# GpSimd's pieces of each head tied to scales, and the order of the hash codes' transfers, in a bucketed attention with two expert layers

## The chip, the cores and the metric

The kernel runs on one core of one Trainium2 chip. The metric is the device time of one execution in microseconds (us). TensorE is PE in the rows, VectorE is DVE, ScalarE is ACT, GpSimd is POOL, and SyncE, which issues nearly all transfers, is SP.

## The reference, cut to what matters

Sixteen attention heads (2 batches of 8, 768 tokens, 64 wide) come first. A query may attend only to keys of its own bucket; the bucket is the sign pattern of six projections. Two expert layers follow.

```python
q_bits = (np.einsum('bhsd,dk->bhsk', q, proj) > 0)   # k_bits likewise
mask = q_bucket[:, :, :, None] == k_bucket[:, :, None, :]
scores = np.where(mask, scale * np.matmul(q, k.T), -1e9)
attn = softmax(scores); attn_out = np.matmul(attn, v)
x = moe(attn_out)            # top-1 of 8 experts, relu, gates
return (x @ w_a) * (x @ w_b) @ w_out
```

## The kernel before

The program is written out by hand: within an engine, instructions run in the order of the code. The attention loop runs over `g`, 96 steps of one head `h` (0 to 15) and one tile `t` (0 to 5) of 128 queries. Step `g` issues the scores of tile `g + 1` (`scores`, L183 and L184: for each half of the keys one matmul with the rounded values and the codes, `tq` and `tk`, and one with the corrections, `bq` and `bk`), then `smax` on VectorE: a minimum over the scores in PSUM (L189, `mm`) and a two-input instruction that makes from it the scale and bias of the exponential (L190, `sb`; "a scale" below). ScalarE takes the exponential (L198, `p`), TensorE transposes it in two halves (L211, `tp`), and ScalarE or VectorE copies each half out (`pt`, L215 and L217). The product with the values (`av`, L226) and the output step of an older head (`o_out`, L265 to L293: matmul `m`, then `lp`, `xf` or `x_b` on VectorE) lie between.

`side(pos)` is called three times in a step (positions 0, 1, 2). It makes the operands of coming heads at places that the table `K` gives as pairs (tile, position). For a head two ahead: `split_a` rounds on ScalarE (`tq`, `tk`, L110), `split_b` makes the corrections. Of the queries, the first half is a VectorE instruction (`bq`, L123) and the second a GpSimd cast (L127). Of the keys, the first half is a GpSimd subtraction (`bk`, L129) and the second a GpSimd cast (L130). GpSimd has more work: the sums of the router's logits (`lg`, L290) and the repacking of the head's output into 16-bit planes (`x_q`, L247, from `to_planes` and `late_planes`), both at the end of `o_out` in tile 4. A `held` copy (L842, L845) reads the newest scale, so that what follows it on GpSimd starts only when that scale is made. Before, the query cast at (5, 2) stands behind one, and the key subtraction at (2, 2) behind none.

The codes: eight small matmuls (L149) give the projections of the next head, one VectorE instruction (L164, `code`) compares them, and `hash_codes` (L159 to L172) sends the result in eight transfers of 9 KB from SP's queue into twelve rows of `tq` and `tk` (L171), four for the queries and then four for the keys. In heads 0 and 1 it is four transfers of 18 KB. From step 62 on a list `todo` gives VectorE one piece of the first batch's router per step (`s1`, `s1b`, ...: L316 to L398), directly behind `smax`; from head 11 tile 3 on it holds the six scatters of the first batch (L482, `xr`), issued by GpSimd. While heads 14 and 15 run, `extra` hands GpSimd pieces of the expert layer, each behind a held copy (L744, L753).

Of the kernel before, what the change touches and what calls it, by code (L numbers as in the profile page):

```python
# [7 lines left out]
F32 = mybir.dt.float32  # L8
# [7 lines left out]
ALU = mybir.AluOpType  # L16
# [5 lines left out]
S, D, NB, NH = 768, 64, 2, 8  # L22
# [1 line left out]
N, DM, E, FF, F2 = 1536, 512, 8, 1024, 1536  # L24
C = 224
GR = ((0, 6), (6, 4), (10, 2))
K = {'se': (2, 0, 2, 0, 2, 0), 'se0': (0, 1, 2, 1, 1, 2), 'ev': (0, 0, 0, 1, 0, 1, 0, 0, 0, 0, 1, 0), 'ev0': (0, 0, 0, 1, 0, 1, 0, 0, 0, 1, 0, 0), 'ev1': (0, 0, 0, 1, 0, 1, 0, 0, 0, 1, 0, 1), 'avl': (5,), 'oul': 0, 'hml': 0, 'hc': ((0, 0), (0, 2), (1, 1), (2, 1)), 'sa': (None, (2, 2)), 'sb': ((1, 0), (2, 2)), 'sa0': ((2, 2), (4, 1)), 'sb0': ((3, 2), (5, 0)), 'hm0': 0, 'hc0': ((1, 0), (1, 2), (3, 0), (4, 1))}
C_ID, C_TRI, C_THR, C_REV, C_TOK, C_IOTA, C_BASE, C_SLOT = 0, 128, 256, 258, 266, 278, 279, 287
CW = C_SLOT + C
FAR = 1024.0  # L30
# [4 lines left out]
def attn_moe_kernel(ctx: ExitStack, tc: tile.TileContext, xin, cst, projd, wblk, wmoe, w2in, out):  # L35
    nc = tc.nc
    PE, ACT, DVE, POOL = nc.tensor, nc.scalar, nc.vector, nc.gpsimd
# [22 lines left out]
    lg = const.tile([128, 12, 16], F32, name="lg")  # L60
# [3 lines left out]
    pos = const.tile([128, 12], F32, name="pos")  # L64
# [25 lines left out]
    NHD = NB * NH  # L90
    X, XT, V, T, B, PT = {}, {}, {}, {}, {}, {}
    st, pt_ = {}, {}
    scl, nbs, last = {}, {}, {}
# [20 lines left out]
    def split_b(h, i, lo=0, n=S, parts=(0, 1)):  # L114
        copy = POOL.tensor_copy if h or i else ACT.copy
        x = X[h][:, i * S + lo:i * S + lo + n]
        if (h, i) not in B:
            B[h, i] = tb.tile([128, S], F32R, tag="b" + "qk"[i], name="b" + "qk"[i])
        b = B[h, i][:, lo:lo + n]
        t = T[h, i].bitcast(F32)[:, lo:lo + n]  # L120
        if i == 0:
            if 0 in parts:
                DVE.scalar_tensor_tensor(  # L123
                    out=b[:64], in0=x[:64], scalar=-0.125, in1=t[:64], op0=ALU.mult, op1=ALU.subtract
                )
            if 1 in parts:
                copy(b[64:], t[64:])  # L127
        else:
            (POOL if h else DVE).tensor_tensor(out=b[64:], in0=x[64:], in1=t[64:], op=ALU.subtract)  # L129
            copy(b[:64], t[:64])  # L130

    hp_ = {}

# [27 lines left out]
    def hash_codes(h):  # L161
        n = 192 if h > 1 else 384
        c = sm.tile([128, n], F32R, tag="code" if h > 1 else "o", name="code", bufs=1 if h > 1 else 2)
        DVE.tensor_scalar(  # L164
            out=c, in0=hp_[h, 0][:, :n], scalar1=thr[:, 0:1], scalar2=thr[:, 1:2], op0=ALU.is_gt, op1=ALU.mult
        )
        for j in range(4):
            i, k = divmod(j, 2)
            for r in range(384 // n):
                at = r * 384 + k * n  # L170
                nc.sync.dma_start(  # L171
                    out=T[h, i].bitcast(F32)[64:76, at:at + n],  # L172
                    in_=c.bitcast(F32)[32 * j + 12 * r:32 * j + 12 * r + 12],
                )

    def scores(g):
# [64 lines left out]
    def halves(ap):  # L241

        return ap.bitcast(U16).rearrange("p t (n a) -> p t a n", a=2)

    def to_planes(t0, nt, hh, src):
        o = x_q.bitcast(U16).rearrange("p t (a n) -> p t a n", a=2)[:, t0:t0 + nt, :, hh * 64:(hh + 1) * 64]
        POOL.tensor_copy(o, src)  # L247

    def late_planes(hh, t0=0, nt=6):
        to_planes(t0, nt, hh, halves(x_b)[:, t0:t0 + nt, :, hh * 64:(hh + 1) * 64])  # L250

    oT, rs = {}, {}

    def o_evac(h, q=None, copy=DVE.tensor_copy):
        n = q[1] * 128 if q else 384
# [9 lines left out]
    def o_out(h, q=None):  # L265
        b, hh = divmod(h, NH)
        o, r = oT.pop((h, q)), rs.pop((h, q))
        p = ps_m.tile([128, 512], F32, tag="m", name="m")
        t0, nt = q or (0, NT)
        t = slice(b * 6 + t0, b * 6 + t0 + nt)  # L270
        lp = sm.tile([128, nt, 16], F32, tag=f"lp{nt}", name="lp", bufs=2) if hh else lg[:, t]
        if b:
            xo = x_b[:, t0:t0 + nt, hh * 64:(hh + 1) * 64]
        else:
            xf = xo = sm.tile([128, 6, 64], F32, tag="xf", name="xf", bufs=1)
        if q is None:
            for j in range(3):
                PE.matmul(p[:, j * 160:(j + 1) * 160], o[:, j * 128:(j + 1) * 128], wb[:, hh], start=True, stop=True)
            ps = p[:, :480].rearrange("p (j c n) -> p j c n", j=3, c=2)
            rr = r.rearrange("p (c j) -> p j c", c=2).unsqueeze(3)  # L280
            lo, xo, sh = lp.rearrange("p (c j) n -> p j c n", c=2), xo.rearrange("p (c j) n -> p j c n", c=2), [128, 3, 2]
        else:
            for j in range(nt):
                PE.matmul(p[:, j * 80:(j + 1) * 80], o[:, j * 128:(j + 1) * 128], wl, start=True, stop=True)
            ps = p[:, :nt * 80].rearrange("p (j n) -> p j n", j=nt)
            rr, lo, sh = r[:, :nt].unsqueeze(2), lp, [128, nt]
        DVE.tensor_tensor(out=lo, in0=ps[..., 64:], in1=rr.to_broadcast(sh + [16]), op=ALU.mult)
        DVE.tensor_tensor(out=xo, in0=ps[..., :64], in1=rr.to_broadcast(sh + [64]), op=ALU.mult)
        if hh:
            (DVE if hh >= NH - 2 else POOL).tensor_tensor(out=lg[:, t], in0=lg[:, t], in1=lp, op=ALU.add)  # L290
        if not b:
            to_planes(0, 6, hh, halves(xf))
        elif NH + 3 <= h < L:  # L293
            late_planes(hh)

    def router(gi):
        t0, n = GR[gi]
# [362 lines left out]
    with tc.manual_schedule():  # L660
# [19 lines left out]
        for r, c in ((0, 0), (64, 12)):  # L680
            p = pst[r:r + 64]
            DVE.tensor_copy(p[:, c + 38:c + 44], p[:, c:c + 6])
            for to in (6, 32):
                DVE.tensor_scalar(
                    out=p[:, c + to:c + to + 6], in0=p[:, c:c + 6], scalar1=-1.0, scalar2=None, op0=ALU.mult
# [53 lines left out]
        held = sm.tile([128, 1], F32, tag="held", name="held", bufs=1)  # L739
        L = NHD - 1  # L740
# [29 lines left out]
        for g in range(NG):  # L770
# [57 lines left out]
            def side(pos):  # L828
                if (t, pos) == (5, 0) and h and h + 3 < NHD:
                    split_a(h + 3, 0)  # L830
                if g + 1 < NG and K["se" if 0 < h < L else "se0"][t] == pos:
                    sexp(g + 1)
                if h < L and (t, pos) == (1, 0):
                    hash_codes(h + 1)
                    if 0 < h < L - 1:
                        load_halves(h + 2)
                for i in range(2):
                    if h + 2 < NHD and K["sa" if h > 1 else "sa0"][i] == (t, pos):
                        split_a(h + 2, i)
                    if h + 2 < NHD and K["sb" if h > 1 else "sb0"][i] == (t, pos):  # L840
                        if t == 5:
                            POOL.tensor_copy(held, last[0])  # L842
                        split_b(h + 2, i, parts=(0,) if h > 1 and i == 0 else (0, 1))
                if (t, pos) == (5, 2) and h and h + 3 < NHD:
                    POOL.tensor_copy(held, last[0])  # L845
                    split_b(h + 3, 0, parts=(1,))

            side(0)
            tposes(g, 0)
# [694 lines left out]
```

## Time and profile before

| | us |
|---|---|
| median of 3 runs | 726.84 (726.68 to 727.46) |
| the profiled execution | 729.09 |
| its span, first to last instruction | 727.3 |
| TensorE busy | 705.2 |
| VectorE busy | 554.6 |
| ScalarE busy | 448.9 |
| GpSimd busy | 276.2 |

The profile is of one execution. Times in its rows run from the first instruction. A row of the timeline is a start, a length, the engine, the line of the kernel, the operation, what it writes and reads, the shape and a count; a bracket behind it is the idle time of the engine just before and what ended it. Rows that follow each other may be merged into one with a count. Matmuls are pipelined, so their lengths overlap, and the distance of starts says more than the length. The attention stage lasts until about 262 us, and the granted clock of TensorE is 1.00 in each of its stretches.

### The profile page before, as it was taken

The numbers are of one execution on the slowest core, as the hardware profiler recorded it, in microseconds if no ns is written. First come the engines' busy times: TensorE is split into PE (matmuls) and PEld (weight loads), VectorE is DVE, ScalarE is ACT, GpSimd is POOL, SyncE is SP. The second block draws the span as 40 slices with busy tenths as digits, with TensorE's granted clock in tenths as the row PEclk, the third lists the DMA queues.
The fourth block names the chain that finished last, engine by engine and source line by source line (L and its number), as shares of the span: only waits on it lengthen the run. The fifth ranks groups of instructions, "written<-read, shape, count | busy, mean of one in ns | idle before, by whom it ended". The sixth has DMA issues, their size and how long they took to land.

```text
span 727.3 us, 13315 instructions
## 1 busy us (share of the span) xinstructions
PE 705.2 (97%) x4505; PEld 602.5 (83%) x4506; DVE 554.6 (76%) x1108; ACT 448.9 (62%) x962; POOL 276.2 (38%) x328
## 2 busy tenths in 40 slices
PE   8899999999999999999999999999999999999995
PEld 6666776776666588999999999999999999999994
DVE  6777777778777787788888878886887877777644
ACT  5887788777777536677778766566443453444320
POOL 4342233222445447854454303234322333223234
PEclk9999999999999999999999999999999999999998
DMA  7345465542331039699899741133211222121013
GB/s 246 110 140 197 155 227 183 171 140 82 125 93 48 30 122 249 162 243 229 217 288 252 245 133 35 54 115 88 59 58 59 87 68 79 50 67 59 0 57 120
DMA packets 57017, 93.52 MB, mean 129 GB/s; under 512 B 20864, under 2 KB 25072, under 8 KB 56944
## 3 DMA queue, kind: packets, MB, share of 16 engines
q1 hardware_dynamic: 54192, 86.12, 40.3%
q0 software_dynamic: 2304, 6.31, 2.3%
q8 instruction: 37, 0.61, 0.3%
q14 instruction: 36, 0.29, 0.1%
q10 hardware_dynamic: 448, 0.20, 0.1%
HBM read 75.16 MB, written 13.12 MB: 121 GB/s over the span
## 4 chain that ended last, share of the span: by engine, by line
PE 73%; DVE 5%; POOL 5%; issue 5%; DMA 5%; SPq 3%; ACT 3%; ACTq 0%; DVEq 0%; POOLq 0%
PE tp L211 6%; PE av L226 6%; PE y L1071 5%; PE aba L1308 3%; PE abb L1308 3%; PE aba L1310 3%; PE aba L1309 3%; PE s L183 3%; PE abb L1310 3%; PE abb L1309 3%; PE h L1033 3%; PE h L1032 3%; PE h L1031 3%; SPq L171 3%; PE s L184 3%
## 5 line engine op out<-in xcount | busy, mean ns | idle before, releaser
L189 DVE TENSOR_REDUCE mm<-s 128x1 f32<-128x768 f32 x96 | 91.1, 949 | 29.0 <-PE s L184 27.3
L198 ACT ACTIVATE p<-s,sb 128x768 f32<-128x768 f32 x96 | 95.0, 990 | 24.1 <-DVE sb L190 21.3
L211 PEld LDWEIGHTS tp<-cs,p 128*128 128x128 f32 x576 | 64.0, 140 | 40.1 <-ACT p L198 24.8
L211 PE MATMUL tp<-cs,p 128*128 128x128 f32 x576 | 82.4, 279 | 7.3 <-ACT p L198 4.1
L539 DVE TENSOR_TENSOR wl<-wr,wh 128x512 fp32r<-128x512 f32 x125 | 82.1, 697 | 4.6 <-ACT wh L538 0.8
L215 ACT ACTIVATE pt<-tp 128x384 f32<-128x384 f32 x143 | 65.1, 488 | 32.6 <-PE tp L211 32.6
L1002 POOL TENSOR_TENSOR pc<-t,pc 128x256 fp32r<-128x256 f32 x38 | 32.8, 865 | 134.9 <-ACT pc L1001 119.8
L1071 PE MATMUL y<-hl,wh 128*128 128x448 f32 x224 | 75.1, 378 | 1.0 <-DVE hl L1045 0.9
L183 PE MATMUL s<-tk,tq 76*128 76x384 f32 x192 | 74.0, 385 | 1.8 <-DMA tk<-code 0.8
L538 ACT ACTIVATE wh<-wr 128x512 fp32r<-128x512 f32 x128 | 73.5, 624 | 0.6 <-DMA wr<-wmoe 0.5
L1031 PE MATMUL h<-xh,wh 128*128 128x224 f32 x256 | 70.4, 275 | 1.0 <-ACT xh L1027 0.8
L1032 PE MATMUL h<-xl,wh 128*128 128x224 f32 x256 | 70.4, 275 | 0.6 <-DVE xl L1028 0.3
L1033 PE MATMUL h<-xh,wl 128*128 128x224 f32 x256 | 70.6, 276 | 0.0
L226 PE MATMUL av<-pt,v 128*64 128x384 f32 x360 | 68.0, 499 | 0.2 <-DVE r L261 0.2
L184 PE MATMUL s<-bk,bq 128*128 128x384 f32 x192 | 65.2, 339 | 0.0
L129 POOL TENSOR_TENSOR bk<-x,tk 64x768 fp32r<-64x768 f32 x15 | 27.3, 1820 | 90.9 <-ACT tk L110 90.6
L1072 PE MATMUL y<-hl,wl 128*128 128x224 f32 x224 | 59.6, 266 | 0.0
L1031 PEld LDWEIGHTS h<-xh,wh 128*128 128x128 f32 x256 | 49.0, 191 | 2.4 <-ACT xh L1027 1.0
L1002 POOL TENSOR_TENSOR pc<-s,pc 128x256 fp32r<-128x256 f32 x44 | 37.8, 869 | 33.1 <-ACT pc L1001 31.4
L952 ACT ACTIVATE x<-r 128x512 uint8<-128x512 uint8 x36 | 28.5, 793 | 34.7 <-DVE x L949 34.7
L1032 PEld LDWEIGHTS h<-xl,wh 128*128 128x128 f32 x256 | 49.2, 192 | 0.9 <-DVE xl L473 0.5
L1198 ACT ACTIVATE gh<-p 128x384 fp32r<-128x384 f32 x21 | 11.0, 526 | 62.6 <-DVE p L1327 62.6
(266 smaller groups left out, 1982.0 us busy)
## 6 DMA issues: line engine op xcount, KB each, us to landing
wr<-wmoe SPq DMA_DIRECT2D x128, 256.0 KB
r<-w2in SPq DMA_DIRECT2D x36, 512.0 KB
x<-xin SPq DMA_DIRECT2D x30, 384.0 KB
xr<-zero SPq DMA_DIRECT2D x13, 512.0 KB
xt<-xin SPq DMA_DIRECT2D x14, 384.0 KB
v<-xin SPq DMA_DIRECT2D x16, 192.0 KB
tq<-code SPq DMA_DIRECT2D x56, 9.0 KB
tk<-code SPq DMA_DIRECT2D x56, 9.0 KB
```

The source lines that it names most:

```text
L183: PE.matmul(p[:, c, :384], T[h, 0][:76, qs], T[h, 1][:76, sl], start=True, stop=False)
L184: PE.matmul(p[:, c, :384], B[h, 0][:, qs], B[h, 1][:, sl], start=False, stop=True)
L189: DVE.tensor_reduce(out=m[:, 1:2], in_=st[g][:, :, :384], axis=AX.XY, op=ALU.min)
L198: ACT.activation(p.rearrange("p (c n) -> p c n", c=2), st.pop(g)[:, :, :384], ACTF.Exp, scale=scl.pop(g), bias=nbs.pop(g), accum_out=sums[ ...
L211: PE.transpose(ps[:, j * 128:(j + 1) * 128], pt_[g][:, k * 128:(k + 1) * 128], ident)
L226: PE.matmul(av[h][c * 64:(c + 1) * 64, :384], v, PT[h][:, k, c * 384:(c + 1) * 384], start=(k == 0), stop=(k == NT - 1), skip_group_check= ...
L538: ACT.activation(h, r, ACTF.Copy)
L539: eng.tensor_tensor(out=l, in0=r, in1=h.bitcast(F32), op=ALU.subtract)
L1031: PE.matmul(ps, wh, xh, start=first, stop=False)
L1032: PE.matmul(ps, wh, xl, start=False, stop=False)
L1033: PE.matmul(ps, wl, xh, start=False, stop=last)
L1071: PE.matmul(p, wh[:, w], hl, start=(f == 0), stop=False, skip_group_check=True)
```

## The change

It has two parts.

The transfers of the codes: the four of the keys go first. Of the queries' four, those for columns 0 to 191 and 192 to 383 follow and those for 384 to 575 and 576 to 767 are last. Their number and size stay.

GpSimd's pieces: from head 2 on, the subtraction for the keys moves from (2, 2) to (3, 0), behind a held copy. The keys' cast, which followed it at once, moves to (4, 0), behind a held copy of its own, and the sum of the logits follows it. The repacking of the output moves from tile 4 to (5, 2), behind the held copy there and ahead of the queries' cast; heads 0 and 1 get that held copy too. From head 13 on, sums and repacking stay in `o_out`.

```diff
-'sb': ((1, 0), (2, 2))
+'sb': ((1, 0), (3, 0))
...
         else:
-            (POOL if h else DVE).tensor_tensor(out=b[64:], in0=x[64:], in1=t[64:], op=ALU.subtract)
-            copy(b[:64], t[:64])
+            if 0 in parts:
+                (POOL if h else DVE).tensor_tensor(out=b[64:], in0=x[64:], in1=t[64:], op=ALU.subtract)
+            if 1 in parts:
+                copy(b[:64], t[:64])
...
-        for j in range(4):
-            i, k = divmod(j, 2)
-            for r in range(384 // n):
+        for j in (2, 3, 0, 1) if n == 384 else (2, 3, 0, 1, 4, 5):
+            i, k = divmod(j % 4, 2)
+            for r in (range(384 // n) if j in (2, 3) else (j // 4,)):
...
+        add, turn = [], []
         if hh:
-            (DVE if hh >= NH - 2 else POOL).tensor_tensor(out=lg[:, t], in0=lg[:, t], in1=lp, op=ALU.add)
+            add = [lambda: (DVE if hh >= NH - 2 else POOL).tensor_tensor(out=lg[:, t], in0=lg[:, t], in1=lp, op=ALU.add)]
         if not b:
-            to_planes(0, 6, hh, halves(xf))
+            turn = [lambda: to_planes(0, 6, hh, halves(xf))]
         elif NH + 3 <= h < L:
-            late_planes(hh)
+            turn = [lambda: late_planes(hh)]
+        if h < NHD - 3:
+            adds.extend(add)
+            turns.extend(turn)
+        else:
+            for f in add + turn:
+                f()
...
-                        if t == 5:
+                        if (t, i) in ((5, 1), (3, 1)):
                             POOL.tensor_copy(held, last[0])
-                        split_b(h + 2, i, parts=(0,) if h > 1 and i == 0 else (0, 1))
-                if (t, pos) == (5, 2) and h and h + 3 < NHD:
+                        split_b(h + 2, i, parts=(0,) if h > 1 else (0, 1))
+                if 1 < h < NHD - 2 and (t, pos) == (4, 0):
                     POOL.tensor_copy(held, last[0])
-                    split_b(h + 3, 0, parts=(1,))
+                    split_b(h + 2, 1, parts=(1,))
+                    if adds:
+                        adds.pop()()
+                if (t, pos) == (5, 2) and h < L:
+                    POOL.tensor_copy(held, last[0])
+                    for f in adds + turns:
+                        f()
+                    adds.clear()
+                    turns.clear()
+                    if h and h + 3 < NHD:
+                        split_b(h + 3, 0, parts=(1,))
```

What stands in a row, at three places. First SP's queue, one steady head (`x` and `v` are a later head's inputs, `xt` the input of the code matmuls, `xr<-zero` a clearing of memory). Before:

```order
L98 DMA x<-xin 128x768 x2
L100 DMA v<-xin 128x384
L171 DMA tq<-code 12x192 x4
L171 DMA tk<-code 12x192 x4
L105 DMA xt<-xin 128x768
L782 DMA xr<-zero 256x1x512 x2
```

The same place after:

```order
L98 DMA x<-xin 128x768 x2
L100 DMA v<-xin 128x384
L173 DMA tk<-code 12x192 x4
L173 DMA tq<-code 12x192 x4
L105 DMA xt<-xin 128x768
L791 DMA xr<-zero 256x1x512 x2
```

Only the two groups of four have changed places.

Second GpSimd, one steady head. Before:

```order
L845 COPY held<-sb 128x1
L127 CAST bq<-tq 64x768
L129 TENSOR_TENSOR bk<-x,tk 64x768
L130 CAST bk<-tk 64x768
L290 TENSOR_TENSOR lg<-lg,lp 128x96
L247 COPY x_q<-xf 128x12x64
```

After:

```order
L859 COPY held<-sb 128x1
L249 COPY x_q<-xf 128x12x64
L127 CAST bq<-tq 64x768
L851 COPY held<-sb 128x1
L130 TENSOR_TENSOR bk<-x,tk 64x768
L854 COPY held<-sb 128x1
L132 CAST bk<-tk 64x768
L293 TENSOR_TENSOR lg<-lg,lp 128x96
```

Two held copies are new, subtraction and cast are parted by one of them, and the repacking stands ahead of the queries' cast.

Third GpSimd from the end of head 10 to head 12, where the scatters begin (`L482 DMA xr` before, `L491 DMA xr` after). Before:

```order
L845 COPY held<-sb 128x1
L127 CAST bq<-tq 64x768
L129 TENSOR_TENSOR bk<-x,tk 64x768
L130 CAST bk<-tk 64x768
L482 DMA xr<-x_q,pos_i 3328x512
L290 TENSOR_TENSOR lg<-lg,lp 128x96
L482 DMA xr<-x_q,pos_i 3328x512
L845 COPY held<-sb 128x1
L127 CAST bq<-tq 64x768
L482 DMA xr<-x_q,pos_i 3328x512
L129 TENSOR_TENSOR bk<-x,tk 64x768
```

After:

```order
L859 COPY held<-sb 128x1
L127 CAST bq<-tq 64x768
L491 DMA xr<-x_q,pos_i 3328x512
L851 COPY held<-sb 128x1
L130 TENSOR_TENSOR bk<-x,tk 64x768
L854 COPY held<-sb 128x1
L132 CAST bk<-tk 64x768
L293 TENSOR_TENSOR lg<-lg,lp 128x96
L491 DMA xr<-x_q,pos_i 3328x512
L859 COPY held<-sb 128x1
L127 CAST bq<-tq 64x768
L491 DMA xr<-x_q,pos_i 3328x512 x2
```

The first scatter now stands ahead of head 11's subtraction, and two scatters stand ahead of head 12's.

## Rows read from the trace of the kernel before

**Rows 1.** Windows by head: length; PE, PEld, DVE, ACT, POOL busy; clock; DMA.

```profile
41.81:56.09 14.28, 14.28 (x100) 10.21 (x99) 10.95 (x23) 11.46 (x23) 5.46 (x8) 1.00 0.57 185
56.09:70.95 14.86, 14.48 (x100) 10.20 (x99) 10.98 (x23) 11.56 (x23) 4.85 (x6) 1.00 0.51 168
...
158.99:175.22 16.23, 14.71 (x108) 10.43 (x107) 13.90 (x29) 11.68 (x23) 3.65 (x4) 1.00 0.28 91
175.22:191.42 16.20, 14.75 (x100) 10.21 (x99) 13.04 (x30) 11.49 (x23) 5.35 (x6) 1.00 0.37 122
```

**Rows 2.** Timeline of PE: scores inside a head, then at two heads' starts.

```profile
55.45 0.34 PE L184 MATMUL s<-bk,bq 128*128 128x384 f32 x1
55.64 0.34 PE L183 MATMUL s<-tk,tq 76*128 76x384 f32 x1
...
65.38 0.34 PE L184 MATMUL s<-bk,bq 128*128 128x384 f32 x1
66.11 0.42 PE L183 MATMUL s<-tk,tq 76*128 76x384 f32 x1 [0.38 <-DMA tk<-code]
...
229.94 0.34 PE L184 MATMUL s<-bk,bq 128*128 128x384 f32 x1
230.38 0.41 PE L183 MATMUL s<-tk,tq 76*128 76x384 f32 x1
```

**Rows 3.** Chain that ended last (start, length, what): the last code transfer.

```profile
107.52 0.71 SPq L171
108.28 1.83 DMA tk<-code
```

**Rows 4.** Timeline of PE: the two long stalls, heads 10 and 11.

```profile
169.12 0.93 PE L211 MATMUL tp<-cs,p 128*128 128x128 f32 x6 [1.52 <-ACT pt L215]
...
185.52 0.93 PE L211 MATMUL tp<-cs,p 128*128 128x128 f32 x6 [1.44 <-ACT pt L215]
```

**Rows 5.** Timeline of DVE: scales, a router instruction, the scatter's addresses.

```profile
109.12 0.48 DVE L190 SCALAR_TENSOR_TENSOR sb<-mm 128x2 f32<-128x2 f32 x1
...
165.73 1.76 DVE L190 SCALAR_TENSOR_TENSOR sb<-mm 128x2 f32<-128x2 f32 x1
...
167.64 0.78 DVE L322 TENSOR_TENSOR oh<-rt_cd,rt_cm 128x48 bf16<-128x48 f32 x1
...
180.45 0.17 DVE L386 TENSOR_TENSOR pos_i<-pos,rt_p 128x6 int32<-128x6 f32 x1
...
182.08 1.81 DVE L190 SCALAR_TENSOR_TENSOR sb<-mm 128x2 f32<-128x2 f32 x1
...
188.26 0.16 DVE L190 SCALAR_TENSOR_TENSOR sb<-mm 128x2 f32<-128x2 f32 x1
```

**Rows 6.** Timeline of POOL: a query cast, a key subtraction, a scatter and its waiter.

```profile
112.41 0.83 POOL L127 CAST bq<-tq 64x768 fp32r<-64x768 f32 x1
...
165.65 1.82 POOL L129 TENSOR_TENSOR bk<-x,tk 64x768 fp32r<-64x768 f32 x1 [8.35 <-ACT tk L110]
...
186.66 0.99 POOL L482 DMA_INDIRECT xr<-x_q,pos_i  x1 [0.17 <-issue]
...
192.37 0.82 POOL L127 CAST bq<-tq 64x768 fp32r<-64x768 f32 x1 [3.70 <-DMA xr<-x_q,pos_i]
```

**Rows 7.** Timeline of DVE across a steady head's start.

```profile
111.94 0.16 DVE L190 SCALAR_TENSOR_TENSOR sb<-mm 128x2 f32<-128x2 f32 x1
112.80 0.56 DVE L217 COPY pt<-tp 128x384 f32<-128x384 f32 x1 [0.69 <-PE tp L211]
```

**Rows 8.** Timeline of ACT at the same place: exponentials of tiles 0 and 1.

```profile
112.22 0.99 ACT L198 ACTIVATE p<-s,sb 128x768 f32<-128x768 f32 x1 [0.45 <-DVE sb L190]
...
115.31 0.99 ACT L198 ACTIVATE p<-s,sb 128x768 f32<-128x768 f32 x1 [0.28 <-DVE sb L190]
```

**Rows 9.** Timeline of PE at the same place: their transposes.

```profile
113.64 0.82 PE L211 MATMUL tp<-cs,p 128*128 128x128 f32 x6
...
117.00 0.88 PE L211 MATMUL tp<-cs,p 128*128 128x128 f32 x6
```

More of the change, by code (lines that the diff above doesn't have):

```diff
@@ L26 @@
 GR = ((0, 6), (6, 4), (10, 2))
-K = {'se': (2, 0, 2, 0, 2, 0), 'se0': (0, 1, 2, 1, 1, 2), 'ev': (0, 0, 0, 1, 0, 1, 0, 0, 0, 0, 1, 0), 'ev0': (0, 0, 0, 1, 0, 1, 0, 0, 0, 1, 0, 0), 'ev1': (0, 0, 0, 1, 0, 1, 0, 0, 0, 1, 0, 1), 'avl': (5,), 'oul': 0, 'hml': 0, 'hc': ((0, 0), (0, 2), (1, 1), (2, 1)), 'sa': (None, (2, 2)), 'sb': ((1, 0), (2, 2)), 'sa0': ((2, 2), (4, 1)), 'sb0': ((3, 2), (5, 0)), 'hm0': 0, 'hc0': ((1, 0), (1, 2), (3, 0), (4, 1))}
+K = {'se': (2, 0, 2, 0, 2, 0), 'se0': (0, 1, 2, 1, 1, 2), 'ev': (0, 0, 0, 1, 0, 1, 0, 0, 0, 0, 1, 0), 'ev0': (0, 0, 0, 1, 0, 1, 0, 0, 0, 1, 0, 0), 'ev1': (0, 0, 0, 1, 0, 1, 0, 0, 0, 1, 0, 1), 'avl': (5,), 'oul': 0, 'hml': 0, 'hc': ((0, 0), (0, 2), (1, 1), (2, 1)), 'sa': (None, (2, 2)), 'sb': ((1, 0), (3, 0)), 'sa0': ((2, 2), (4, 1)), 'sb0': ((3, 2), (5, 0)), 'hm0': 0, 'hc0': ((1, 0), (1, 2), (3, 0), (4, 1))}
 C_ID, C_TRI, C_THR, C_REV, C_TOK, C_IOTA, C_BASE, C_SLOT = 0, 128, 256, 258, 266, 278, 279, 287
@@ L172, in hash_codes @@
                     out=T[h, i].bitcast(F32)[64:76, at:at + n],
-                    in_=c.bitcast(F32)[32 * j + 12 * r:32 * j + 12 * r + 12],
+                    in_=c.bitcast(F32)[32 * (j % 4) + 12 * r:32 * (j % 4) + 12 * r + 12],
                 )
@@ L250, in late_planes @@
         to_planes(t0, nt, hh, halves(x_b)[:, t0:t0 + nt, :, hh * 64:(hh + 1) * 64])
-    oT, rs = {}, {}
+    oT, rs, adds, turns = {}, {}, [], []
     def o_evac(h, q=None, copy=DVE.tensor_copy):
```

## The prediction

> **What bounds the kernel now.** I read first the windows cut at the code matmul of each head, then TensorE's timeline in the long heads, then who was late there. In a good head TensorE has no free time: 14.28 us long, 14.28 us busy, with VectorE at 10.95 and ScalarE at 11.46 [rows 1]. So only what makes a head longer than 14.28 can be won, and only in the attention stage. Two kinds of loss stand out.
>
> The first is at the start of a head. The third score matmul of tile 0, the first that reads the second half of the keys' codes, follows its forerunner by 0.73 us where 0.19 is usual, and what ended the wait is a transfer of `tk` codes [rows 2]. The head around that row is 14.86 us long [rows 1]; nine heads' starts have such a loss.
>
> The second is in heads 10 and 11, 16.23 and 16.20 us long [rows 1]. In each TensorE stands idle once before a transpose, 1.52 and 1.44 us [rows 4]. The row names a `pt` copy as the releaser, but the transpose needs the exponential `p`, and that needs the scale. The scale at that point takes 1.76 and 1.81 us instead of 0.16 [rows 5, 7]. In head 10 GpSimd's subtraction for the keys started 0.08 us ahead of it, at 165.65, and ends at 167.47; the scale ends at 167.49 [rows 5, 6]. So a scale that comes while GpSimd computes waits until the GpSimd instruction is done. In steady heads the same happens with the shorter cast, 0.48 us [rows 5], and TensorE loses nothing there. Copies out of PSUM are not held: one of 0.56 us runs beside a cast [rows 6, 7].
>
> **The change part by part.** *The codes.* The code transfers leave SP's queue 0.76 us apart, and the last lands 1.83 us after its issue [rows 3]. Before, the first scores of a head need the seventh transfer (columns 0 to 383 of the keys' codes) and the eighth. After, they need the four of the keys and the fifth; the built program has them wait for these five alone, and the sixth to eighth are waited for by later tiles. The last one that tile 0 needs thus comes 3 x 0.76 = 2.3 us earlier. The largest loss at a head's start is under 0.6 us, so all of them should go, with 1.7 us to spare. Their size: measured on the starts of the score matmuls, the nine losses, from 0.54 at 66.11 (0.73 - 0.19) to 0.25 at 230.38 (0.44 - 0.19) [rows 2], add up to 3.0. The bounds are 0 and 9 times the first head's 0.58 (14.86 - 14.28 [rows 1]), 5.2; the sum of what was measured is the value to take. What is late next is nothing that a row shows: VectorE and ScalarE have 3 us free in such a head [rows 1]. Heads 0 and 1 have no code wait and win nothing. The queue's other transfers keep their places.
>
> *The subtraction behind a scale.* In head 10 the subtraction would start about 0.3 us after the scale ends (a held copy and the start; between scale and cast at 111.94 and 112.41 it is 0.47 from start to start [rows 6, 7]). The scale is then free, and the 1.52 us go [rows 4]. Two scales of a steady head are 2.8 us apart (109.12 and 111.94 [rows 5, 7]), and the subtraction lasts 1.82 [rows 6], so it fits between them. I put down 1.5; bounds 0 (it meets the next scale instead) and 1.9 (16.23 - 14.28 [rows 1]).
>
> In head 11 the scale is freed as well, 1.4 us [rows 4], but the subtraction now stands behind the first scatter, and the built program has it wait for the scatter's landing. Addresses are ready at 180.6 [rows 5], so the scatter is issued at 180.8 or so. From issue to the next waiting instruction's start took 5.7 us for the second scatter (186.66 to 192.37 [rows 6]), my nearest row. So the subtraction would run at about 186.5 to 188.3 instead of 182.05. The next scale is that of head 12's tile 0, at 188.26 [rows 5], which without the stall comes 1.4 us sooner, at 186.9. It would be held for some 1.4 us. What of that reaches TensorE: at a steady start the scale ends at 112.10, the exponential starts 0.12 later and is done at 113.2, and the transpose starts at 113.64 [rows 7 to 9], which leaves 0.4. So up to 1.0 us comes back; if the scatter lands sooner or later than the scale, none. I put down 0.6, hence 0.8 gained in head 11. Bounds: 1.4 and 0.
>
> In head 12 the subtraction waits for two scatters in the same way and may meet another scale; before, its cast waited likewise and TensorE lost nothing that I can see. I put down 0.2 lost, bounds 0 and 1.6.
>
> *The other pieces.* The new held copies lie on GpSimd, which is busy 4.85 us in 14.86 [rows 1]: nothing, as long as it has that much free time. The cast behind the next scale removes the 0.48 us scale [rows 5], worth nothing since TensorE did not wait. Repacking and query cast behind head `h + 1`'s first scale take 2 x 0.83 [rows 6] and end some 2.1 us behind it; the next exponential is 3.1 us behind the first (112.22 and 115.31 [rows 8]). Readers of all these operands come a head or more later, and the load of a later head's `x`, which waits in SP's queue for the subtraction, is delayed in heads 11 and 12 alone, a full head before its use. In the last two heads GpSimd's list only changes the place of one sum and one repacking; I put down nothing.
>
> **A rule against it.** The row first: the router instruction `oh` in head 10, a VectorE instruction with two inputs, took 0.78 us from 167.64, while the keys' cast ran behind the subtraction that ended at 167.47 [rows 5, 6]; its end, 168.42, is about one cast (0.83 [rows 6]) later. The router stands directly behind the scale, and so, after the change, does the subtraction. The Trainium skill (GPSIMD Engine Reference, section 8, Key points) says that GpSimd contends with VectorE instructions with two SBUF inputs or in a two-port mode. By that rule, with which the trace agrees on `oh`, the pieces right behind a scale can hold the router's instructions instead of the scale. By the rule head 10's 1.5 could be lost and the sum be 3.6; without it the sum is 5.1 as below. The third rival works the mechanism out from rows.
>
> **The sum.** 3.0 + 1.5 + 0.8 - 0.2 = 5.1 us. The profiled execution took 729.09 us, a span of 727.3 and 1.8 around it; 729.09 - 5.1 = 724.0. It was 2.25 us above the median of the runs, and the median becomes 726.84 - 5.1 = 721.7. Behind the attention stage everything follows from its end, and transfers are nearly idle there, so I expect the gain to pass through whole.
>
> **The rivals.**
> 1. *All clean.* No scatter hits a scale, and heads 10 and 11 fall to 14.28 as well: 3.0 + (16.23 + 16.20 - 2 x 14.28) = 6.9, so 719.9. For: GpSimd has much free time. Against: the router's own work makes VectorE busier there, 13.90 and 13.04 [rows 1], of which only 1.6 each is the held scale.
> 2. *Codes alone.* In heads 11 and 12 the subtractions behind the scatters each hold a later scale by up to 1.65 us with little slack, and this takes back heads 10 and 11's gain: 726.84 - 3.0 = 723.8. For: the 5.7 us of a scatter.
> 3. *The router held.* In head 10 the last router instruction waits for the subtraction, up to 1.8 us, and the minimum for the next scale behind it. The exponential there has about as much slack as that, so the price is 0 to 1.5, at most head 10's whole gain: 723.2.
> 4. *The codes' part does nothing*, because another need of tile 0 is as late as the codes: 5.1 - 3.0 = 2.1, so 724.7. For: three engines meet there. Against: heads without the loss run at 14.28.
> 5. *Slower.* The long GpSimd run behind each head's first scale (repacking, then cast, to 2.1 us behind it) holds VectorE's `pt` copy, from 112.80 to about 114.2. The exponential of tile 1 would move from 115.31 by 1.4 us; it has 117.00 - 116.4 = 0.6 before its transpose [rows 7 to 9], so TensorE loses 0.8 in each of heads 2 to 13: 9.6 - 5.1 = 4.5, and 731.3. It decides from a delay of 0.6 us and cancels the gain at 1.0. Against: a copy out of PSUM beside a cast took 0.56 as always.
>
> **How the numbers follow.** Forecast 0.53, all clean 0.13, codes alone 0.17, router held 0.08, codes do nothing 0.05, slower 0.04. A range of 719.5 to 724.3 takes in the first four, with 0.4 below the all-clean case for code losses up to the first head's size in more heads, and leaves out the last two, 0.09, and parts of the others' spread. A measurement tells about 0.2% (1.45 us) from no change, so faster is below 725.4: all cases but the last, less 0.06 for terms that are all too large at once. Faster 0.90, same 0.06, slower 0.04.
>
> **What would show it.** Codes: third score matmuls 0.19 us behind their forerunners at every head's start, no wait on code transfers, windows of heads 3 to 9 at 14.3. Subtraction: no scale over 0.5 us in heads 2 to 10, head 10 near 14.5. Scatters: a wait of the subtraction on `xr` in head 11 and a long scale at the start of head 12. I am wrong if heads 3 to 9 stay above 14.5, if the `pt` copies grow longer beside repacking, or if a new wait appears between attention and the experts.

## The result and the profile after

| | us | ratio to before, 95% |
|---|---|---|
| before, its runs beside the changed kernel | 727.15 (726.68 to 728.83) | |
| after | 721.25 (720.43 to 722.83) | 0.9917 (0.9894 to 0.9941) |
| after, a second set of runs (a1 below) | 721.38 (719.91 to 721.77) | 0.9915 (0.9897 to 0.9934) |
| forecast | 721.7 (719.5 to 724.3) | |

The change makes the kernel 5.9 to 6.2 us faster. The profiled execution took 722.83 us with a span of 721.0, against 729.09 and 727.3. The rows below are windows cut, as in [rows 1], at the code matmul of each head: length, busy time of PE, PEld, DVE, ACT and POOL, clock, DMA. They are heads 3, 6, 10, 11, 12 and 13 of the changed kernel, then all behind the last of these windows. The code matmul stands in tile 1 of a head, so a window runs from there to tile 1 of the next head, and the first scores of that next head lie in it.

```profile
56.14:70.38 14.24, 14.24 (x100) 10.26 (x99) 10.66 (x23) 11.44 (x23) 5.08 (x8) 1.00 0.49 165
...
98.84:113.56 14.72, 14.48 (x100) 10.28 (x99) 10.68 (x23) 11.54 (x23) 5.08 (x8) 1.00 0.79 259
156.28:171.00 14.72, 14.72 (x108) 10.44 (x108) 12.12 (x30) 11.65 (x23) 3.97 (x6) 1.00 0.30 100
171.00:185.63 14.63, 14.59 (x99) 10.20 (x98) 11.45 (x30) 11.50 (x23) 5.66 (x8) 1.00 0.32 85
185.63:199.88 14.25, 14.25 (x100) 10.26 (x99) 10.68 (x23) 11.43 (x23) 7.28 (x10) 1.00 0.39 126
199.88:214.89 15.01, 14.45 (x99) 10.23 (x99) 11.32 (x24) 10.81 (x22) 6.47 (x9) 1.00 0.21 65
214.89:721.00 506.11, 494.25 (x3067) 454.11 (x3066) 387.06 (x767) 280.24 (x627) 200.74 (x232) 1.00 0.42 118
```

Head 13 of the kernel before, for which [rows 1] have no line:

```profile
205.84:220.42 14.58, 14.48 (x100) 10.19 (x99) 11.25 (x24) 10.81 (x22) 5.65 (x6) 1.00 0.17 51
```

Beside [rows 1]: head 3 fell from 14.86 to 14.24, head 10 from 16.23 to 14.72, head 11 from 16.20 to 14.63. Heads 2 to 9 are at 14.24, where TensorE is busy throughout, but for head 6. Head 13 is the one that grew, from 14.58 to 15.01. Together heads 1 to 13 went from 193.22 to 187.53 us, 5.7 of the span's 6.3. The rest lies behind them, 506.88 before and 506.11 after. Of that 0.3 us is the ninth code wait, at 230.38 in [rows 2]: from the last code matmul to the expert stage's first product it is 43.82 us before (220.42 to 264.24) and 43.48 after (214.89 to 258.37). What differs behind that product is no gain: in the twelve profiles of this study this part lasts 501.7 to 506.9 us whatever the kernel (501.7 is e8, whose end of attention is about 1.0 us shorter). Of the 2.2 us between the two profiles of the changed kernel all arises at 277 to 300 us, where the expert stage's first products wait. So the heads are the thing to compare, and a single profiled time is uncertain by 2 us or so.

**The codes.** The first scores in the window of head 3, which stand beside 65.38 and 66.11 in [rows 2], on TensorE's timeline after:

```profile
65.17 0.42 PE L185 MATMUL s<-tk,tq 76*128 76x384 f32 x1
65.44 0.34 PE L186 MATMUL s<-bk,bq 128*128 128x384 f32 x1
65.62 0.34 PE L185 MATMUL s<-tk,tq 76*128 76x384 f32 x1
```

The third matmul follows 0.18 us behind the second, and no wait on a code transfer is left there.

**Head 10.** VectorE and GpSimd around the scale that took 1.76 us in [rows 5]:

```profile
163.10 0.16 DVE L192 SCALAR_TENSOR_TENSOR sb<-mm 128x2 f32<-128x2 f32 x1
...
163.41 0.23 DVE L331 TENSOR_TENSOR oh<-rt_cd,rt_cm 128x48 bf16<-128x48 f32 x1
163.56 0.20 DVE L332 TENSOR_TENSOR ohl<-cs,rt_cm 128x48 bf16<-128x48 f32 x1
...
165.19 0.31 DVE L192 SCALAR_TENSOR_TENSOR sb<-mm 128x2 f32<-128x2 f32 x1
```

```profile
163.40 0.19 POOL L851 COPY held<-sb 128x1 f32<-128x1 f32 x1 [7.98 <-DVE rt_cm L330]
163.66 1.82 POOL L130 TENSOR_TENSOR bk<-x,tk 64x768 fp32r<-64x768 f32 x1
```

The scale takes 0.16 us, `oh` 0.23 and not 0.78, and the subtraction runs from 163.66 to 165.48. The two scales are only 2.09 us apart here, so it reaches 0.3 us into the second, which then takes 0.31. TensorE does not notice. What head 10 has over 14.24 is mostly the router's own matmuls.

**Head 11.** The first scatter, the subtraction that stands behind it, and VectorE's scales:

```profile
177.39 1.15 POOL L491 DMA_INDIRECT xr<-x_q,pos_i  x1 [8.39 <-DMA tk<-code]
...
180.52 1.83 POOL L130 TENSOR_TENSOR bk<-x,tk 64x768 fp32r<-64x768 f32 x1 [1.74 <-DVE lp L289]
...
183.87 1.01 POOL L491 DMA_INDIRECT xr<-x_q,pos_i  x1 [0.16 <-issue]
...
189.56 0.83 POOL L127 CAST bq<-tq 64x768 fp32r<-64x768 f32 x1 [4.48 <-DMA xr<-x_q,pos_i]
```

```profile
180.18 0.16 DVE L192 SCALAR_TENSOR_TENSOR sb<-mm 128x2 f32<-128x2 f32 x1
...
182.49 0.16 DVE L192 SCALAR_TENSOR_TENSOR sb<-mm 128x2 f32<-128x2 f32 x1
```

The subtraction waits 1.74 us. The row names `lp`, but the scatter's packets end at 179.95, and 0.5 to 0.6 us from the last packet to the waiting instruction is what the study's other scatters show too. It ends at 182.35, and the next scale starts at 182.49: free by 0.14 us. From issue to waiter it took 3.1 us for this scatter, and 5.7 for the second (183.87 to 189.56), as in [rows 6]. What differs is what else was being moved. Windows of after behind each issue, up to about the scatter's first packet (the last two numbers are the busy share of the DMA engines and GB/s):

```profile
177.40:179.10 1.70, 1.70 (x14) 1.61 (x13) 0.58 (x2) 1.31 (x2) 1.32 (x2) 1.00 0.05 11
183.90:186.50 2.60, 2.60 (x25) 1.84 (x25) 2.46 (x7) 1.87 (x4) 1.17 (x2) 1.00 0.84 229
```

At 182.37, as soon as the subtraction is done, SP's queue starts the load of a later head's inputs; the first scatter goes out before it, the second into it.

**Head 13**, the one that grew: GpSimd, VectorE and TensorE.

```profile
198.26 1.02 POOL L491 DMA_INDIRECT xr<-x_q,pos_i  x1 [0.16 <-issue]
...
202.09 0.83 POOL L127 CAST bq<-tq 64x768 fp32r<-64x768 f32 x1 [2.61 <-DMA xr<-x_q,pos_i]
```

```profile
202.27 1.46 DVE L123 SCALAR_TENSOR_TENSOR bq<-x,tq 64x768 fp32r<-64x768 f32 x1
203.66 0.54 DVE L219 COPY pt<-tp 128x384 f32<-128x384 f32 x1
```

```profile
204.25 0.55 PE L213 MATMUL tp<-cs,p 128*128 128x128 f32 x3 [0.56 <-DVE pt L219]
```

The query cast waits for the scatter ahead of it and starts at 202.09, just before VectorE's two-input half of a coming head's queries. That half is held and takes 1.46 us instead of the 0.94 it has where no cast lies beside it; the `pt` copy behind it is late, and TensorE stands 0.56 us.

### The profile page after: what moved, and what is told of

Its sections match the earlier page's. It is cut to its first block, busy times and chain, and to the rows that moved or that the text cites. A ratio compares the mean times of both kernels' runs of the same rounds, so it can differ in the third digit from the quotient of the medians.

```text
span 721.0 us, 13387 instructions
## 1 busy us (share of the span) xinstructions
PE 702.4 (97%) x4505; PEld 603.2 (84%) x4506; DVE 548.0 (76%) x1108; ACT 448.3 (62%) x962; POOL 280.9 (39%) x355
## 4 chain that ended last, share of the span: by engine, by line
PE 81%; POOL 5%; issue 4%; DVE 4%; ACT 3%; DMA 1%; ACTq 0%; POOLq 0%; DVEq 0%
PE tp L213 9%; PE av L228 8%; PE y L1090 5%; PE s L185 4%; PE s L186 4%; PE aba L1327 3%; PE h L1052 3%; PE aba L1329 3%; PE aba L1328 3%; PE abb L1327 3%; PE abb L1329 3%; PE abb L1328 3%; PE h L1051 3%; PE h L1050 3%; PE q L1257 3%
## 5 line engine op out<-in xcount | busy, mean ns | idle before, releaser
L1052 PEld LDWEIGHTS h<-xh,wl 128*128 128x128 f32 x256 | 49.1, 192 | 0.0
```

The source lines that it names most:

```text
L1052: PE.matmul(ps, wl, xh, start=False, stop=last)
```

## The experiments

All times are medians; a ratio is to runs of the kernel before on the same chip. "Heads" is the length of heads 1 to 13 in the one profiled execution: 193.22 before, 187.53 and 186.88 in the two profiles of after.

| run | us | ratio, 95% | heads |
|---|---|---|---|
| e1: code order alone | 723.59 | 0.9957 (0.9942 to 0.9973) | 189.90 |
| e2: pieces alone | 725.39 | 0.9982 (0.9965 to 0.9998) | 191.51 |
| e3: subtraction alone moved | 724.72 | 0.9967 (0.9951 to 0.9983) | 192.52 |
| e4: after without new held copies | 722.77 | 0.9948 (0.9931 to 0.9965) | 189.07 |
| e5: after, subtraction twice | 730.77 | 1.0061 (1.0045 to 1.0078) | 195.53 |
| e6: after, scatters moved | 720.58 | 0.9903 (0.9885 to 0.9921) | 186.67 |
| e7: after, weights moved | 721.35 | 0.9915 (0.9896 to 0.9935) | 187.15 |
| e8: after, last head's piece moved | 719.18 | 0.9903 (0.9887 to 0.9920) | 187.66 |
| e9: e6, e7 and e8 together | 719.44 | 0.9884 (0.9865 to 0.9903) | 187.10 |

### The two parts alone

e1 is the kernel before with the loop over the code transfers of the changed kernel; e2 is the changed kernel with the old loop:

```diff
-        for j in range(4):
-            i, k = divmod(j, 2)
-            for r in range(384 // n):
+        for j in (2, 3, 0, 1) if n == 384 else (2, 3, 0, 1, 4, 5):
+            i, k = divmod(j % 4, 2)
+            for r in (range(384 // n) if j in (2, 3) else (j // 4,)):
```

> The kernel before with the new order of the code transfers and nothing else. The two-part theory (waits on codes at nine heads' starts, and scales held by GpSimd in heads 10 and 11, each worth its own microseconds) expects the waits of heads 2 to 9 and 13 gone but for head 6, where the transfers stand behind expert weights, and the stalls of heads 10 and 11 as before: 2.5 to 3.0 us under the kernel before, ratio about 0.996. The rival, that another need of the first scores is as late as the codes and only both parts together win, expects under 1 us (0.999 or more).

> The changed kernel with the old order of the code transfers. The two-part theory expects the windows of heads 3 to 9 as long as before (14.4 to 15.0 us), those of heads 10 and 11 at 14.6 to 14.8 instead of 16.2, and a new stall of some 0.7 us in head 13: 2.5 to 3.3 us under the kernel before, ratio about 0.996. The rival (each part worth little without the other) expects under 1 us.

Windows of e1, heads 3, 10 and 11, and on TensorE's timeline of e2 the code wait that is back in the window of head 3:

```profile
55.61:69.85 14.24, 14.24 (x99) 10.26 (x98) 10.99 (x23) 11.45 (x23) 4.86 (x6) 1.00 0.50 164
...
155.55:171.79 16.24, 14.72 (x108) 10.44 (x108) 13.91 (x29) 11.64 (x23) 3.65 (x4) 1.00 0.28 91
171.79:187.97 16.18, 14.74 (x99) 10.20 (x98) 13.02 (x30) 11.48 (x23) 5.35 (x6) 1.00 0.38 121
```

```profile
65.62 0.42 PE L185 MATMUL s<-tk,tq 76*128 76x384 f32 x1 [0.41 <-DMA tk<-code]
```

The parts are separate. The codes alone clear the heads' starts (3.3 us in the heads, 3.1 by the ratio) and leave heads 10 and 11 as they were. The pieces alone leave the code waits and take 1.3 us by the ratio, less than expected: heads 10 to 12 are 15.01, 15.19 and 15.22 us there. The two add up to 4.4 us where both together give 6.0. That the pieces are worth more beside clean starts isn't shown: each ratio is uncertain by over 1 us, and in e2's profile three things make heads 10 to 12 longer than after's, by 1.8 us in all. In head 10 a code wait of 0.27 comes out that the long stall had hidden. In head 11 the keys' cast starts at 184.57, just ahead of a scale at 184.62, which takes 0.79 us; in head 12 the subtraction starts just ahead of a scale. Both pieces come behind a wait for a scatter, and e8 below shows that such hits come and go with the new code order too. (That the wait for a code goes in head 6 as well was not expected of e1.)

### The subtraction alone, and the pieces without their waits

e3 is the kernel before with only the subtraction moved behind the scale, the cast right behind it; e4 is the changed kernel without the two new held copies:

```diff
-'sb': ((1, 0), (2, 2))
+'sb': ((1, 0), (3, 0))
...
-                        if t == 5:
+                        if (t, i) in ((5, 1), (3, 1)):
```

```diff
-                        if (t, i) in ((5, 1), (3, 1)):
+                        if (t, i) == (5, 1):
...
-                    POOL.tensor_copy(held, last[0])
                     split_b(h + 2, 1, parts=(1,))
```

> The kernel before with one GpSimd piece moved: the keys' subtraction goes to tile 3 behind a held copy, its cast directly behind it; sums, repacking and code transfers stay. If only the two scales held by the subtraction cost TensorE time, this gives the whole gain of the GpSimd part: heads 10 and 11 at 14.6 to 14.9 us and 2.5 to 3.3 us under the kernel before (ratio 0.996). If tying the other pieces to scales matters as well, it gives less than two thirds of what the pieces together give, under 2 us.

> The changed kernel without the held copies ahead of the keys' subtraction and ahead of the keys' cast; the pieces keep their new places in GpSimd's list. If the alignment with the scale is what helps, the subtraction in head 10 starts when ScalarE's rounding is done, as before, and holds the scale there for up to 1.8 us: head 10 at 16 us, and the kernel 1.4 to 1.8 us slower than the changed one (head 11's subtraction also waits for a scatter, so its stall need not return), about 722.9, ratio 0.994. If the new place in GpSimd's list is enough, head 10 stays at 14.7 and the time at 721.3 (0.992).

e4's GpSimd and VectorE in head 10, and TensorE behind them:

```profile
162.65 1.82 POOL L130 TENSOR_TENSOR bk<-x,tk 64x768 fp32r<-64x768 f32 x1 [7.52 <-ACT tk L110]
```

```profile
162.72 1.76 DVE L192 SCALAR_TENSOR_TENSOR sb<-mm 128x2 f32<-128x2 f32 x1
...
164.63 0.78 DVE L331 TENSOR_TENSOR oh<-rt_cd,rt_cm 128x48 bf16<-128x48 f32 x1
```

```profile
166.12 0.93 PE L213 MATMUL tp<-cs,p 128*128 128x128 f32 x6 [1.52 <-ACT pt L217]
```

Without the held copy the subtraction starts when ScalarE's rounding of `tk` is done, 0.07 us ahead of the scale, and the whole loss of head 10 is back, 16.24 us. That shows what removes it: not a different order on GpSimd, but the wait for the scale. Head 11's loss does not come back (14.86), since there the scatter decides when the subtraction starts. e4's head 12 is 15.01, with a subtraction released by a scatter and a scale of 1.53 us, and its head 13 only 14.24, so its time agrees with the expectation for more reasons than head 10. e3 gains no less than e2 by the ratio, though their intervals overlap, and it has neither the moved repacking nor a cast parted from the subtraction, so the subtraction is what the second part is about. Its heads 10 and 11 were expected at 14.6 to 14.9 and are 15.16 and 15.00; 0.4 of that in head 10 is a code wait. In e2 and e3 the loss moved to head 12, 15.22 and 15.33 us: there the scatters release the subtraction at 197.02 and 198.98, and the scales at 197.13 and 198.99 take 1.73 and 1.83 us. (e3's profile was 1.3 us over its median, by longer code waits in heads 3 and 6.)

### The hold measured by itself

e5 does the subtraction twice in a row:

```diff
-            if 0 in parts:
+            for _ in range((2 if h > 3 else 1) if 0 in parts else 0):
                 (POOL if h else DVE).tensor_tensor(out=b[64:], in0=x[64:], in1=t[64:], op=ALU.subtract)
```

> GpSimd does the keys' subtraction twice in a row, the second time with the same result, in heads 2 to 13: 3.64 us behind the scale of tile 4 instead of 1.82. In the changed kernel's trace a subtraction starts at 120.36, the scale of tile 5 at 122.47 and its transposes at 124.93. The doubled one ends at 124.0. Theory: the scale of tile 5 is held until then, takes about 1.7 us instead of 0.16, and the transposes come 1.63 us behind its end, which is what lay between the end of a held scale and the transposes in the kernel before (167.49 to 169.12); that is 125.6, 0.7 us late in each of 12 heads, so about 8.4 us more than the changed kernel, 729.7. Rival: the exponentials' slack at tile 5 swallows the hold, and the time stays at 721.3. Second rival: VectorE is not held by GpSimd at all and the long scales had another cause; then the scale stays at 0.16 us and the time too.

GpSimd, VectorE and TensorE in head 7 of e5:

```profile
124.29 3.71 POOL L130 TENSOR_TENSOR bk<-x,tk 64x768 fp32r<-64x768 f32 x2
```

```profile
126.40 1.62 DVE L192 SCALAR_TENSOR_TENSOR sb<-mm 128x2 f32<-128x2 f32 x1
```

```profile
129.25 0.87 PE L213 MATMUL tp<-cs,p 128*128 128x128 f32 x6 [0.32 <-ACT p L200]
```

The scale waits until GpSimd is done, to 128.02 against 128.00, and the kernel is slower than before. The heads cost 8.0 us more than after's, 8.4 expected; by the ratios it is 10.5. The steps differ from the expectation in both directions: the transposes come 1.23 us behind the scale and not 1.63, yet a second tile is late as well, so heads 3 to 7 are 15.10 instead of 14.24, and heads 8 and 9 are 15.7. Both rivals are out. In head 11 of the same run GpSimd and VectorE are:

```profile
188.91 3.71 POOL L130 TENSOR_TENSOR bk<-x,tk 64x768 fp32r<-64x768 f32 x2 [2.35 <-DMA xr<-x_q,pos_i]
```

```profile
190.27 0.47 DVE L192 SCALAR_TENSOR_TENSOR sb<-mm 128x2 f32<-128x2 f32 x1
```

The first of the two subtractions in the row ends at 190.72, and the scale that started at 190.27 takes only 0.47, although the second subtraction runs on from 190.80. So the hold lasts to the end of the one GpSimd instruction that is running, not of the row of them. The Trainium skill (SBUF — State Buffer, "SBUF: two separate sides") says that the pair of ports that the two engines share is an exclusive lock, kept for the whole instruction by whoever starts first; these lengths agree with it.

### Three stalls that are left

e6 moves the six scatters to steps that were meant to have no waiter directly behind them (two casts and a subtraction still wait for one); e7 issues the expert weights two steps later, behind the codes; e8 puts GpSimd's half of a rounding of the expert stage behind a scale; e9 does all three.

```diff
-                for f in r["sc"]:
-                    todo += [f, None]
+                sc = r["sc"]
+                todo += [None, sc[0], None, sc[1], sc[2], None, None, sc[3], None, sc[4], sc[5], None]
```

```diff
-            if g in (6 * NT, 9 * NT):
-                for n in range(3) if g == 6 * NT else (3,):
+            if g in (6 * NT + 2, 9 * NT + 2):
+                for n in range(3) if g == 6 * NT + 2 else (3,):
```

```diff
-            (1, 1): [split_behind(2)],
-            (1, 2): [behind(lambda: w_split(1, 0, POOL))],
+            (1, 1): [lambda: parts.append(x_split(2))],
+            (1, 2): [behind(lambda: parts.pop()()), lambda: w_split(1, 0, POOL)],
```

> The changed kernel once more, beside the others on the same chip. Expected is its first ratio, 0.992 (0.989 to 0.994), and the same stalls in its trace: about 0.5 us of a code wait at the start of head 6, 0.5 us in heads 10 and 11 each, and 0.7 us in head 13.

> The six scatters move to steps where nothing that waits for them follows at once on GpSimd. Theory: head 13 is 0.7 us too long because its query cast waits on GpSimd for the scatter ahead of it and VectorE's half of the queries is held by that cast; with the scatters moved head 13 falls from 15.0 to 14.3 us and the time is 0.7 us below the changed kernel's, a ratio to the kernel before near 0.991. Rival: the loss belongs to the cast's length and not to the scatter; then head 13 stays at 15.0 and the time is unchanged. If a scatter in its new place meets another scale, a head of 11 to 13 grows by up to 1.6 us instead.

> The loads of the expert weights move two steps later, behind the codes in SP's queue. Theory: the one code wait that is left, 0.48 us at the start of head 6, comes from the six 256 KB weight loads that stand ahead of the codes' packets; it goes, head 6 falls from 14.7 to 14.24 us and the time is 0.5 us below the changed kernel's. Rival: the wait comes from the codes' own issue, five transfers 0.76 us apart; then the stall stays at 0.5 us and nothing changes. If the weights meet another head's inputs instead, a wait of 0.3 to 0.6 us appears at the start of head 7.

> The changed kernel with one piece of the expert layer moved: GpSimd's half of a rounding near the end of the attention stage goes behind a scale instead of beside it. Theory: in the changed kernel it starts 0.5 us ahead of a scale, which takes 1.32 us, and TensorE stands 0.85 us; behind the scale it holds nothing, the 0.85 us go, and the time is 0.85 us below the changed kernel's, 720.4, a ratio to before of 0.990. Rival: the expert stage waits at its start for data that come no sooner, and nothing is won.

> Three moves together: the scatters away from what waits for them, the weights behind the codes, and GpSimd's half of the last head's rounding behind a scale instead of beside it. Theory: each removes one stall of TensorE that the trace of the changed kernel shows (0.7 us in head 13, 0.48 us in head 6, 0.85 us near the end of attention), 2.0 us in all, hence 719.2 us by the first times, and a ratio to the changed kernel of 0.997. Rival: the stalls near the end overlap with the join of the expert stage's data, so the last 0.85 us come back there and the gain is 1.2 us or less.

Head 13 in e6, VectorE's two-input instruction there, e6's first scatter with the cast that waits for it and the window behind its issue, and head 6 of a1, the second profile of the changed kernel:

```profile
199.56:214.06 14.50, 14.47 (x99) 10.24 (x99) 10.77 (x24) 10.81 (x22) 6.24 (x10) 1.00 0.22 70
```

```profile
201.95 0.94 DVE L123 SCALAR_TENSOR_TENSOR bq<-x,tq 64x768 fp32r<-64x768 f32 x1
```

```profile
180.22 1.15 POOL L491 DMA_INDIRECT xr<-x_q,pos_i  x1 [0.29 <-POOL bk L130]
...
186.68 0.83 POOL L127 CAST bq<-tq 64x768 fp32r<-64x768 f32 x1 [3.83 <-DMA xr<-x_q,pos_i]
```

```profile
180.20:183.90 3.70, 3.70 (x25) 2.47 (x24) 2.60 (x6) 3.70 (x8) 2.59 (x5) 1.00 0.91 284
```

```profile
98.78:113.01 14.23, 14.23 (x99) 10.25 (x98) 10.65 (x23) 11.43 (x23) 5.07 (x8) 1.00 0.78 268
```

e6: head 13 is 14.50 instead of 15.01 and 14.86, and the instruction takes 0.94 again: the theory on the scatter and the cast holds (the cast of that head now starts at 198.74 and is done before). Head 12 gives 0.1 us back. The time is 0.8 us below a1's, as expected, though the intervals overlap. The first scatter, moved behind the subtraction, now goes out while the inputs come in, and from issue to waiter it takes 6.5 us instead of 3.1. e7 settles nothing: its head 6 is at 14.24, but so is that of the unaltered kernel in its second profile, so the wait of 0.48 us belongs to one execution and not to the kernel. Of the nine profiles with the new order of the codes it is in one, and what caused it stays open.

e8, and the changed kernel, at the scale near the end of the attention stage; first VectorE and TensorE of after, then VectorE of e8:

```profile
236.88 1.32 DVE L192 SCALAR_TENSOR_TENSOR sb<-mm 128x2 f32<-128x2 f32 x1
```

```profile
238.72 0.95 PE L280 MATMUL m<-wb,o 128*128 128x160 f32 x5 [0.69 <-DVE o L259]
```

```profile
236.95 0.16 DVE L192 SCALAR_TENSOR_TENSOR sb<-mm 128x2 f32<-128x2 f32 x1
```

The scale is free, and TensorE's stall is gone. The rival is in part true: a wait for `hot` ahead of the expert stage grows from 0.18 to 0.48 us. The stage's first product still comes 1.0 us sooner, 42.45 us behind the last code matmul instead of 43.48. The ratio of 0.9903 is what was expected; its interval overlaps the changed kernel's. The same profile shows the collision that the forecast had feared, in head 12 (GpSimd, VectorE, the window):

```profile
194.12 1.82 POOL L130 TENSOR_TENSOR bk<-x,tk 64x768 fp32r<-64x768 f32 x1 [1.78 <-DMA xr<-x_q,pos_i]
```

```profile
194.20 1.75 DVE L192 SCALAR_TENSOR_TENSOR sb<-mm 128x2 f32<-128x2 f32 x1
```

```profile
185.24:200.56 15.32, 14.60 (x100) 10.19 (x99) 12.37 (x23) 11.75 (x24) 7.26 (x10) 1.00 0.36 123
```

Up to there e8 is the changed kernel word for word, and in after's profile the same subtraction came at 194.91, behind the scale of 194.54, and head 12 was 14.25. So whether the piece behind a scatter hits a scale changes from execution to execution, and a hit costs 1.07 us in its head. Head 13 of the same profile:

```profile
200.56:215.06 14.50, 14.47 (x99) 10.24 (x98) 10.71 (x23) 10.56 (x22) 6.05 (x9) 1.00 0.17 51
```

Its scatters have not moved, and yet it is as short as e6's: head 12 ended later, and the query cast, at 200.81, was done before VectorE's half began at 202.95. So the loss of head 13 comes and goes as well, and a hit in head 12 can spare it: the two heads together are 0.6 us longer than in after.

e9 is the fastest in the ratio, 0.9884, 2.3 us under the changed kernel by the ratios and 1.9 by the medians, where 2.0 was expected; the intervals overlap slightly. Its profile shows less: its heads, 187.10, are no shorter than a1's 186.88, since heads 7 and 12 are 14.40 and 14.60. That the weights gave anything of this isn't shown.

## Why the forecast was right, step by step

**The codes: right, a little low.** 3.0 was put down. Reckoned as in the forecast's two examples, by the third matmul against the second, the nine losses add up to 2.4; 3.0 comes out with the fourth against the third put in (0.25 instead of 0.18). Head by head, heads 2 to 9 and 12 got 3.0 us shorter, 3.5 without the one wait in head 6; 0.25 of that, in head 9, is not the codes', since e1 has 14.49 there, and 0.3 behind head 13 come on top. e1 gave 3.3 us in the heads. Head 6, at 14.72 in one of the two profiles, shows one of the forecast's signs of being wrong (above 14.5); why it waited there is open. Nothing else was as late as the codes, as the forecast had argued from the engines' free time; the rival in which this part does nothing is out.

**Head 10: right.** 1.5 put down, 1.5 measured (16.23 to 14.72), and e4 shows that the held copy does it. Its fit was reckoned with a pair of scales 2.8 us apart; the pair at hand is 2.09 apart, and the 0.3 us by which the subtraction overran cost nothing, which the forecast had not worked out. The router, third rival, was not held: the subtraction starts 0.26 us behind the start of its held copy, and `oh` and `ohl` had started by then, at 163.41 and 163.56. In this the Trainium skill's rule on two SBUF inputs (GPSIMD Engine Reference, section 8, Key points) was weighed rightly as a condition and not as a result: it holds where GpSimd is ahead, as `oh` shows in e4 (0.78 us), and here it was not.

**Head 11: the failed step.** 0.8 was put down and 1.57 came. The step is the price of the scatter: 5.7 us, read from a scatter that was issued at 186.66 while a later head's inputs came in (DMA share 0.95 in 184.9 to 188.4). The change moves the first scatter ahead of the subtraction, and the load of those inputs waits for the subtraction; so it went out with a DMA share of 0.05 and took 3.1. It is not that the first of a series is quick: in the kernel before, where the first also went out into that load, its first packet moved 3.5 us behind the issue instead of 1.7, and in e6 the first took 6.5. No run changed the traffic alone, so this is read from the traces: of the first two scatters of the twelve profiles, the ten that went out with a share near 0.05 moved their first packet 1.6 to 2.0 us behind the issue, the fourteen others 2.3 to 3.7. So the subtraction was done 11.35 us into head 11 (182.35 - 171.00) and not 13.1 (188.3 - 175.22), and the give-back of 0.6 did not come. The price of a hit was about right: up to 1.0 us was the forecast for a hold of 1.4, and e2, e3 and e8 show 0.98, 1.09 and 1.08 over 14.24 for holds of 1.6 to 1.7, in head 12. What was wrong is that it was put down as a sure loss in head 11; in after, a1, e7 and e8, alike up to there but for the place of the weights' loads, no profile has a hit in head 11 and one has it in head 12. After missed it by 0.14 us in head 11 and 0.21 in head 12, so that none was paid is in part luck.

**Head 12: 0.2 lost was forecast;** the window went from 14.42 to 14.25, as it did with the codes alone, so the pieces cost nothing in this profile. **Head 13: not in the forecast.** The queries' cast behind a scatter was named only for head 12, and as harmless because the kernel before had the same wait. There the cast of 192.37 [rows 6] was done before VectorE's half of the queries began, at 193.52, and in head 13 the cast of 205.88 before the half at 207.83. The price is 0.4 to 0.6 us (15.01, 14.86 and 15.08 in after, a1 and e7, against 14.50 in e6 and e8).

**The other pieces at nothing: right.** The `pt` copies beside repacking and cast are as long as before. Rows of VectorE and GpSimd of after in head 7, a copy that lies beside both:

```profile
125.51 0.56 DVE L219 COPY pt<-tp 128x384 f32<-128x384 f32 x1 [0.70 <-PE tp L213]
```

```profile
125.07 0.83 POOL L249 COPY x_q<-xf 128x768 uint16<-128x768 uint16 x1
...
125.96 0.83 POOL L127 CAST bq<-tq 64x768 fp32r<-64x768 f32 x1
```

So the slower rival did not happen, and e5 shows the one way in which it could have: by the scale, not by the copy.

**The sum.** 3.0 + 1.5 + 0.8 - 0.2 = 5.1 was forecast; 3.0 + 1.5 + 1.6 - 0.4 = 5.7 is what the heads show. The two terms that were off, head 11 (0.8 more) and head 13 (0.4 less), are of opposite sign, so the total is nearer than its parts, by luck. With the 0.3 us of codes behind head 13 it is 6.0, as the ratio has it. That the gain would pass through whole was argued from transfers that are nearly idle behind attention; in the kernel before that holds for 246 to 262 us (DMA share 0.06) but not for 262 to 440 (0.74 and 0.83). The gain did pass, up to the 2 us by which that part differs between executions.

## What to carry to other kernels

Where a short VectorE instruction with two SBUF inputs stands on the path that bounds the kernel, start GpSimd's instructions by its result, and let none of them run when the next one comes: a subtraction of 1.82 us that began 2.11 us ahead of the next scale (120.36 and 122.47) cost nothing, and two in a row, 3.71 us, cost 0.86 in each of heads 3 to 7. A transfer issued by GpSimd undoes this for what waits for its landing, because that starts when the transfer lands and not when the scale is made; keep such waiters away from it. Of a group of transfers, send first what the first reader needs. When a change moves a transfer to another time, price it by what else is moved then, and not by a row from its old surroundings.

## What was not expected

- A scale of 0.16 us is held to the end of the running GpSimd instruction alone: it took 1.62 to 1.83 us when the instruction started just ahead of it, 0.47 when that was in its last half microsecond, though another GpSimd instruction followed 0.08 us later.
- Scatters of the same shape took 3.1 and 5.7 us from issue to their waiter in after, and 6.5 for the first one in e6. In after the packets of the first last from 179.11 to 179.95, those of the second from 186.52 to 189.06. The slow ones went out while a later head's inputs were loaded (DMA share 0.84 and 0.91 behind the issue, against 0.05); how much of the delay that load makes was not measured by itself.
- What lies behind head 13 lasts from 501.7 to 506.9 us in profiles of kernels that are the same there or nearly so, which is as much as the whole effect of the change.
